# Moving the state products of one attention step behind matmuls of the next layer

## The chip, the core, the metric

One core of a Trainium2 chip runs the whole kernel. The metric is the time of one execution on the device in microseconds (us), as the median of several executions. The profile is one further execution, and its span runs from the first to the last instruction. The engines are called PE (matmuls), DVE (vector), ACT (scalar) and POOL (GpSimd); PSUM is what the kernel calls the memory that its matmuls write (`Sps`, `OK`, `Hps`).

## The reference

A linear attention with decay goes over sequences of 768 rows in blocks and carries a state per head. Its output is the input of a two-layer perceptron with a GELU.

```python
for b in range(nb):                                   # blocks of 64 rows
    intra = einsum('bhic,bhjc->bhij', qb, kb) * Dmask
    intra = einsum('bhij,bhjd->bhid', intra, vb)
    inter = einsum('bhid,bhde->bhie', qb * lam_pow, kv_state)
    out[:, :, sl] = intra + inter
    kv_state = lam_block * kv_state + einsum('bhsd,bhse->bhde', kb_dec, vb)
...
x = out.transpose(0, 2, 1, 3).reshape(B * S, H * D)   # 3072 x 512
return gelu(x @ w_in) @ w_out                          # 512 -> 2048 -> 512
```

## The kernel before

The kernel takes 256 rows of four heads as a step. Steps 0 to 3 make the x of the first 512 rows. Four parts of a step matter here, all on the matmul engine (PE): the scores (`Sps`), the products of k and v that update the state (`OK`, columns 256 and up), the products of v with the masked scores (`PT`), and the products of q with the state `u`. The last two add up x in PSUM, and `x_out` copies it out, half on ACT and half on DVE.

```python
def products(n, s, banks=None, evacuate=True):
    ...
    if n is not None:                 # state products of step n, 16 small matmuls
        ...
    for hp in range(2):               # v with masked scores of step s, 16 small matmuls
        ...
    for c in range(2):                # what the states add, 4 matmuls at step 3
        u = us.pop((s, 0) if c else (s - 2, 1))
        ...
    if evacuate:
        x_out(s, OK)
```

The perceptron's work stands in a queue of pieces, and `fill(n)` issues the next n. For the first 512 rows, the first 16 pieces are four stages of two matmuls each for hidden blocks 0 to 3 (128 of the 2048 hidden columns each). A matmul has 256 columns, so a stage is 8 matmuls. Stages 1 and 2 read the x of steps 0 and 2, stage 3 that of step 1, and stage 4 that of step 3. This is the stretch that the change edits:

```python
update(2, 1, "t")
scores(3)
banks = products(3, None)                      # state products of step 3
cast_win(0, 0, 256, 128, c01)                  # weights of hidden blocks 0, 1 to f16, DVE
cast_win(0, 256, 512, 256, c01, on_act=True)   # blocks 2, 3, ACT
update(3, 0)                                   # new state: DVE, then POOL
causal(3)                                      # mask the scores: DVE
queue_group(0)
fill(8)                                        # stages 1 and 2
cast_win(0, 0, 256, 256, c23, on_act=True)
cast_win(0, 256, 512, 256, c23)
fill(2)                                        # first half of stage 3
products(None, 3, banks, evacuate=False)       # PT, then states
x_out(3, banks[0], nc.vector)
fill(6)                                        # second half of stage 3, stage 4
...
for m in W_SUMS:                               # five sums of w_out weights on DVE
    sum_wout(0, m, DVE)
fill(8)
...                                            # casts of w_out
fill(9)
prep(4)                                        # q of step 4 on DVE, k on ACT
stage_t(4)                                     # transposes of step 4 on PE
```

Of the kernel before, what the change touches and what calls it, by code (L numbers as in the profile page):

```python
# [8 lines left out]
FP32 = mybir.dt.float32  # L9
# [6 lines left out]
def kernel(  # L16
# [12 lines left out]
    P = 128  # L29
    B, H, S, D = q.shape  # L30
    SB = 256
    NSB = S // SB
# [23 lines left out]
    ps_M = ctx.enter_context(tc.tile_pool(name="psM", bufs=6, space=PSUM))  # L56
# [43 lines left out]
    def cast_win(j, lo=0, hi=512, w=256, cs=slice(0, NC), on_act=False):  # L100
        t = wstage[("i", j)]
        for i in range(lo, hi, w):
            dst = w_in16[:, cs, j * 512 + i : j * 512 + i + w]
            src = t[:, cs, i : i + w]
            if on_act:
                pin(nc.scalar.activation(out=dst, in_=src, func=AF.Copy))
            else:
                pin(nc.vector.tensor_copy(out=dst, in_=src))
# [103 lines left out]
    qkT = {}  # L212
# [63 lines left out]
    def half64(i):  # L276
        return slice(64 * i, 64 * i + 64)
# [3 lines left out]
    def scores(n):  # L281
        o = qkT[n]
        Sps = ps_S.tile([P, 2, 2, 2, P], FP32, tag="S", name="Sps")
        for hp in range(2):
            for jk in range(2):
                for hl, c in TILES:
                    pin(nc.tensor.matmul(  # L287
                        Sps[half64(c), hl, hp, jk, :], o[half64(hl), 1, jk, hp, half64(c)],
                        o[half64(hl), 0, :, hp, half64(c)], start=True, stop=True,
                        skip_group_check=True))  # L290
        Ss[n] = Sps

    def causal(n):

        t = ptp.tile([P, 2, 2, 2, P], FP16, tag="PT", name=f"PT_{n}")
        pin(nc.vector.tensor_tensor(  # L296
            t[:].rearrange("p a b c d -> p (a b) (c d)"),
            Ss.pop(n)[:].rearrange("p a b c d -> p (a b) (c d)"),
            mask[:].unsqueeze(1).to_broadcast([P, 4, 2 * P]), ALU.mult))
        PTs[n] = t  # L300

    def products(n, s, banks=None, evacuate=True):


        OK, opened = banks or ([ps_M.tile([P, 512], FP32, tag="M", name=f"OK{c}")
                                for c in range(2)], set())

        def start(c, hl):
            if (c, hl) in opened:
                return False  # L310
            opened.add((c, hl))
            return True

        if n is not None:
            _, tk, tv = a16[n]
            last = (n // 2) % NSB == NSB - 1
            for jk in range(2):
                for hp in range(2):
                    for c, hl in TILES:
                        if c == 1 and last:  # L320
                            continue
                        pin(nc.tensor.matmul(  # L322
                            OK[c][half64(hl), 256 + hp * D : 256 + hp * D + D],
                            tk[half64(c), jk, 2 * hp + hl, :], tv[half64(c), jk, 2 * hp + hl, :],
                            start=start(c, hl), stop=(jk == 1), skip_group_check=True))
            Kps[n] = OK
        if s is None:
            return OK, opened
        sbg, half = divmod(s, 2)
        o = qkT.pop(s)  # L330
        PT = PTs.pop(s)
        _, _, tv = a16.pop(s)
        for hp in range(2):
            for jk in range(2):
                for c, hl in TILES:
                    pin(nc.tensor.matmul(  # L336
                        OK[c][half64(hl), hp * P : hp * P + P], tv[half64(c), jk, 2 * hp + hl, :],
                        PT[half64(c), hl, hp, jk, :], start=start(c, hl), stop=False,
                        skip_group_check=True))
        for c in range(2):  # L340
            if c == 0 and sbg % NSB == 0:
                continue
            u = us.pop((s, 0) if c else (s - 2, 1))
            for hp in range(2):
                pin(nc.tensor.matmul(OK[c][:, hp * P : hp * P + P], u[:, hp].rearrange("p l d -> p (l d)"),  # L345
                                     o[:, 0, :, hp, half64(c)], start=False, stop=True,
                                     skip_group_check=True))
        if evacuate:
            x_out(s, OK)
        return OK, opened  # L350

    def x_out(s, OK, second=None):
        sbg, half = divmod(s, 2)
        g, i = group_of[sbg]
        if g not in xT:
            xT[g] = xtp.tile([P, 2, len(groups[g]), 2, SB], FP16, tag="xT", name=f"xT_{g}")
        dst = xT[g][:, half, i]
        for c in range(2):
            d = dst[:, :, c * P : (c + 1) * P].rearrange("p hp (t j) -> p hp j t", j=2)
            o = OK[c][:, 0:256].rearrange("p (hp j t) -> p hp j t", hp=2, j=2)  # L360
            if c == 1 and second is not None:
                pin(second.tensor_copy(out=d, in_=o))
            else:
                pin(nc.scalar.activation(out=d, in_=o, func=AF.Copy))  # L364
# [3 lines left out]
    def update(s, c, parts="tu"):  # L368


        sbg, half = divmod(s, 2)
        sb = sbg % NSB
        if c == 1 and sb == NSB - 1:
            Kps.pop(s)
            return
        if "t" in parts:
            OK = Kps[s] if c == 0 else Kps.pop(s)
            K = OK[c][:, 256:384].rearrange("p (hp d) -> p hp d", hp=2)
            t = ucp.tile([P, 2, D], FP32, tag=f"t{half}", name=f"t_{s}_{c}")
            if sb == 0 and c == 0:  # L380
                pin(nc.vector.tensor_copy(out=t[:], in_=K))
            else:
                for hp in range(2):
                    pin(nc.vector.scalar_tensor_tensor(  # L384
                        t[:, hp, :], state[half][:, hp, :],
                        lamu[:, 2 * half + hp : 2 * half + hp + 1], K[:, hp, :],
                        ALU.mult, ALU.add))
            state[half] = t
        if "u" in parts:
            u = ubp.tile([P, 2, 2, D], FP16, tag=f"u{half}", name=f"u_{s}_{c}")  # L390
            pin(nc.gpsimd.tensor_tensor(  # L391
                u[:], state[half][:].unsqueeze(2).to_broadcast([P, 2, 2, D]),
                lumask[:, 2 * half : 2 * half + 2, :].unsqueeze(3).to_broadcast([P, 2, 2, D]),
                ALU.mult))
            us[(s, c)] = u
# [196 lines left out]
    def fill(n):  # L592
        for _ in range(min(n, len(filler))):
            filler.pop(0)()

    def R(n, s):
        if n is not None:
            scores(n)
        products(n, s)
        if n is not None:  # L600
            causal(n)
        if s is not None and s % 2 == 1:
            g, i = group_of[s // 2]
            if i == len(groups[g]) - 1 and g > 0:
                queue_group(g)
        if n is not None:
            update(n, 0)
# [18 lines left out]
    prep(2)  # L626
    scores(1)
    products(1, 0)
    causal(1)
    idle(1)  # L630
# [4 lines left out]
    idle(3)  # L635
    scores(2)
    products(2, None)
    update(2, 0)
    causal(2)
# [4 lines left out]
    products(None, 2)  # L644
    update(2, 1, "t")
    scores(3)
    banks = products(3, None)
    c01, c23 = slice(0, 2), slice(2, 4)
    cast_win(0, 0, 256, 128, c01)
    cast_win(0, 256, 512, 256, c01, on_act=True)  # L650
    update(3, 0)
    causal(3)
    queue_group(0)
    fill(8)
    cast_win(0, 0, 256, 256, c23, on_act=True)
    cast_win(0, 256, 512, 256, c23)
    fill(2)
    products(None, 3, banks, evacuate=False)
    x_out(3, banks[0], nc.vector)
    fill(6)  # L660
    update(3, 1, "t")
    cast_win(1, 0, 512, 256, c01)
    cast_win(1, 0, 512, 256, c23)
# [85 lines left out]
```

## Time and profile before

| | kernel before |
|---|---|
| median of 3 | 205.72 us (205.68 to 205.74) |
| span of the profiled execution | 203.7 us |
| PE busy | 196.1 us, 96% |
| PE waits over 0.15 us up to the last matmul | five, 3.8 us together |

PE is nearly always at work. What it waits for in single places, and what stands in those places, decides the time. The lines are in the prediction.

### The profile page before, as it was taken

The numbers are of one execution on the slowest core, as the hardware profiler recorded it, in microseconds if no ns is written. First come the engines' busy times: TensorE is split into PE (matmuls) and PEld (weight loads), VectorE is DVE, ScalarE is ACT, GpSimd is POOL, SyncE is SP. The second block draws the span as 40 slices with busy tenths as digits, with TensorE's granted clock in tenths as the row PEclk, the third lists the DMA queues.
The fourth block names the chain that finished last, engine by engine and source line by source line (L and its number), as shares of the span: only waits on it lengthen the run. The fifth ranks groups of instructions, "written<-read, shape, count | busy, mean of one in ns | idle before, by whom it ended". The sixth has DMA issues, their size and how long they took to land.

```text
span 203.7 us, 5592 instructions
## 1 busy us (share of the span) xinstructions
PE 196.1 (96%) x2324; PEld 128.3 (63%) x2324; DVE 145.3 (71%) x274; ACT 107.6 (53%) x204; POOL 68.4 (34%) x80
## 2 busy tenths in 40 slices
PE   6988999999999999999999999999999999999992
PEld 1556544556875798644688654788554788545882
DVE  5887727877699998929997728996739673136652
ACT  3374778475782573477632477641576431676110
POOL 6594132446576851336134404314412100000000
PEclk9999999999999999999999999999999999999999
DMA  6999999999999999996449993648330003300014
GB/s 173 290 331 386 386 388 373 289 280 303 323 235 230 290 252 170 234 287 170 103 120 249 188 281 101 159 102 133 95 89 0 3 0 103 108 0 0 3 52 155
DMA packets 63945, 37.85 MB, mean 186 GB/s; under 512 B 17584, under 2 KB 59056, under 8 KB 63920
## 3 DMA queue, kind: packets, MB, share of 16 engines
q1 hardware_dynamic: 63088, 36.97, 69.7%
q10 hardware_dynamic: 832, 0.52, 0.9%
q8 instruction: 18, 0.29, 0.6%
q14 instruction: 7, 0.06, 0.1%
HBM read 27.26 MB, written 6.29 MB: 165 GB/s over the span
## 4 chain that ended last, share of the span: by engine, by line
PE 91%; DVE 4%; POOL 1%; issue 1%; ACT 1%; DVEq 0%
PE Hps L419 37%; PE O2ps L434 10%; PE MB L488 8%; PE MA L488 7%; PE MD L488 7%; PE MC L488 4%; PE Sps L287 4%; PE OK L345 3%; PE Hps L534 3%; PE OK L336 3%; PE Tps L258 2%; PE OK L322 1%; DVE PT L296 1%; POOL dq L186 1%; PE idle L152 1%
## 5 line engine op out<-in xcount | busy, mean ns | idle before, releaser
L419 PE MATMUL Hps<-xT,w_in 128*128 128x512 f16 (+1 forms) x416 | 79.1, 347 | 0.0
L423 ACT ACTIVATE gT<-Hps 128x512 f16<-128x512 f32 x88 | 52.1, 597 | 21.9 <-PE Hps L419 21.1
L419 PEld LDWEIGHTS <-w_in 128*128 128x128 f16 x416 | 40.2, 98 | 33.5
L391 POOL TENSOR_TENSOR u<-t,lumask 128x256 f16<-128x256 f32 x40 | 31.3, 789 | 81.2 <-DVE t L384 54.1
L464 DVE TENSOR_TENSOR gs<-gT 128x512 f16<-128x512 f16 (+1 forms) x70 | 36.6, 586 | 10.8 <-ACT gT L423 10.6
L296 DVE TENSOR_TENSOR PT<-Sps,mask 128x1024 f16<-128x1024 f32 x24 | 29.2, 1216 | 16.9 <-PE Sps L287 16.8
L488 PEld LDWEIGHTS <-gs 128*128 128x128 f16 x360 | 34.8, 98 | 4.0
L227 POOL TENSOR_TENSOR v<-v,dv 128x512 f16<-128x512 f32 x24 | 29.0, 1210 | 5.3 <-DMA v<-in_v_dram 1.7
L364 ACT ACTIVATE xT<-OK 128x256 f16<-128x256 f32 x47 | 18.1, 454 | 20.1 <-PE OK L345 16.3
L434 PE MATMUL O2ps<-w_out,gT 128*128 128x512 f16 x96 | 21.9, 379 | 0.0
L495 ACT ACTIVATE m<-MB 128x512 f32<-128x512 f32 x9 | 5.4, 597 | 25.4 <-PE MB L488 25.4
L242 ACT ACTIVATE qk<-k 128x512 f16<-128x512 f32 x24 | 15.0, 626 | 7.0 <-DMA k<-in_k_dram 6.9
L237 DVE TENSOR_TENSOR qk<-q,dq 128x512 f16<-128x512 f32 x23 | 18.4, 799 | 0.0
L488 PE MATMUL MA<-w_sum,gT 128*128 128x256 f16 x144 | 17.5, 273 | 0.1
L488 PE MATMUL MD<-w_sum,gs 128*128 128x256 f16 x136 | 17.5, 273 | 0.0
L488 PE MATMUL MB<-w_out,gs 128*128 128x256 f16 x144 | 17.2, 273 | 0.0
L488 PEld LDWEIGHTS <-gT 128*128 128x128 f16 x144 | 14.0, 98 | 2.8 <-ACT gT L423 0.3
L384 DVE SCALAR_TENSOR_TENSOR t<-t,lamu,OK 128x64 f32<-128x64 f32 x64 | 14.6, 273 | 1.4 <-PE OK L322 0.8
L434 PEld LDWEIGHTS <-gT 128*128 128x128 f16 x96 | 9.2, 98 | 9.9
L499 DVE TENSOR_TENSOR o<-MA,m 128x512 f32<-128x512 f32 x9 | 6.2, 688 | 12.7 <-ACT m L495 12.7
L124 DVE TENSOR_TENSOR w_sum<-wo,wo 128x1024 f16<-128x1024 f32 x6 | 8.8, 1506 | 4.6 <-DMA wo<-in_moe_w_out_dram 4.6
L287 PEld LDWEIGHTS <-qkT 64*64 64x64 f16 x384 | 6.3, 108 | 8.7 <-issue 4.2
(60 smaller groups left out, 168.4 us busy)
## 6 DMA issues: line engine op xcount, KB each, us to landing
q<-in_q_dram SPq DMA_DIRECT2D x24, 256.0 KB, 4.8
k<-in_k_dram SPq DMA_DIRECT2D x24, 256.0 KB, 5.0
v<-in_v_dram SPq DMA_DIRECT2D x23, 256.0 KB, 5.3
out_dram<-o SPq DMA_DIRECT2D x22, 256.0 KB, 4.3
wo<-in_moe_w_out_dram SPq DMA_DIRECT2D x4, 1024.0 KB, 9.1
wi<-in_moe_w_in_dram SPq DMA_DIRECT2D x4, 512.0 KB, 7.8
wi<-in_moe_w_in_dram SPq DMA_DIRECT2D x2, 1024.0 KB, 12.8
v<-in_v_dram ACTq DMA_DIRECT2D x1, 256.0 KB, 4.2
```

Of the source, the lines that this page charges most:

```text
L227: pin(nc.gpsimd.tensor_tensor(wide(tv[:]), ld32[s][2][:], decay(dv, s), ALU.mult))
L237: pin(q_eng.tensor_tensor(wide(tq), q32[:], decay(dq, s), ALU.mult))
L242: pin(nc.scalar.activation(out=wide(tk), in_=k32[:], func=AF.Copy))
L296: pin(nc.vector.tensor_tensor(t[:].rearrange("p a b c d -> p (a b) (c d)"), Ss.pop(n)[:].rearrange("p a b c d -> p (a b) (c d)"), mask[:]. ...
L364: pin(nc.scalar.activation(out=d, in_=o, func=AF.Copy))
L384: pin(nc.vector.scalar_tensor_tensor(t[:, hp, :], state[half][:, hp, :], lamu[:, 2 * half + hp : 2 * half + hp + 1], K[:, hp, :], ALU.mult ...
L391: pin(nc.gpsimd.tensor_tensor(u[:], state[half][:].unsqueeze(2).to_broadcast([P, 2, 2, D]), lumask[:, 2 * half : 2 * half + 2, :].unsqueez ...
L419: pin(nc.tensor.matmul(by_block(Hps[:, i, :]), w_in16[:, c, f * P : (f + 1) * P], x(c), start=(c == 0), stop=(c == NC - 1)))
L423: pin(nc.scalar.activation(out=dst, in_=Hps[:], func=AF.Gelu_apprx_tanh))
L434: pin(nc.tensor.matmul(O2[tau][0][:], gT[:, f % HF, f // HF, tau * P : (tau + 1) * P], w_out16[:, f, :], start=(n == 0), stop=(n == NF - 1)))
L464: pin(nc.vector.tensor_tensor(gsum[m][:, i, :], block(T0, F0, i), block(T1, F1, i), op))
L488: pin(nc.tensor.matmul(dst, lhsT, rhs, start=(i == 0), stop=(i == HF - 1), skip_group_check=True))
```

## The change

The intent is to use two idle moments of PE. The state products of step 3 go behind stage 1, since PE waited 0.73 us in the middle of them. The products with the states go behind the second half of stage 3, so that the states have more time to become ready.

```diff
-    banks = products(3, None)
+    banks = bank_pair()
     c01, c23 = slice(0, 2), slice(2, 4)
     cast_win(0, 0, 256, 128, c01)
     cast_win(0, 256, 512, 256, c01, on_act=True)
-    update(3, 0)
     causal(3)
     queue_group(0)
-    fill(8)
+    fill(4)
+    products(3, None, banks)
+    update(3, 0)
+    fill(4)
     ...
     fill(2)
-    products(None, 3, banks, evacuate=False)
+    products(None, 3, banks, evacuate=False, add_states=False)
+    fill(2)
+    from_states(3, banks[0])
     x_out(3, banks[0], nc.vector)
-    fill(6)
+    fill(4)
```

The rest of the diff splits `products` into the functions that this needs (`bank_pair`, `from_states`) and moves source lines, so L345, L322 and L534 of before are L354, L324 and L540 after.

More of the change, by code (lines that the diff above doesn't have):

```diff
@@ L300, in causal, with bank_pair, products @@
         PTs[n] = t
-    def products(n, s, banks=None, evacuate=True):
-        OK, opened = banks or ([ps_M.tile([P, 512], FP32, tag="M", name=f"OK{c}")
-                                for c in range(2)], set())
+    def bank_pair():
+        return [ps_M.tile([P, 512], FP32, tag="M", name=f"OK{c}") for c in range(2)], set()
+    def products(n, s, banks=None, evacuate=True, add_states=True):
+        OK, opened = banks or bank_pair()
         def start(c, hl):
@@ L328, in products @@
             return OK, opened
-        sbg, half = divmod(s, 2)
-        o = qkT.pop(s)
         PT = PTs.pop(s)
@@ L339, in products, with from_states @@
                         skip_group_check=True))
+        if add_states:
+            from_states(s, OK)
+        if evacuate:
+            x_out(s, OK)
+        return OK, opened
+    def from_states(s, OK):
+        o = qkT.pop(s)
         for c in range(2):
-            if c == 0 and sbg % NSB == 0:
+            if c == 0 and (s // 2) % NSB == 0:
                 continue
@@ L347, in products @@
                                      skip_group_check=True))
-        if evacuate:
-            x_out(s, OK)
-        return OK, opened
     def x_out(s, OK, second=None):
```

## The prediction

> **What bounds the kernel now.** I read the page's busy shares first, then the chain of work that ended last, then every wait of the matmul engine, and last the timelines of 16 to 22 us, the only stretch that the change touches.
>
> The page, busy shares and queues:
>
> ```profile
> PE 196.1 (96%) x2324; PEld 128.3 (63%) x2324; DVE 145.3 (71%) x274; ACT 107.6 (53%) x204; POOL 68.4 (34%) x80
> ...
> PEclk9999999999999999999999999999999999999999
> ...
> q8 instruction: 18, 0.29, 0.6%
> ...
> PE 91%; DVE 4%; POOL 1%; issue 1%; ACT 1%; DVEq 0%
> ```
>
> PE is busy 96% of the span at full clock, and 91% of the chain is PE. So only a PE hole that is closed can shorten the run, and one opened lengthens it. The waits of PE, in us:
>
> ```profile
> PE idle L152 <- DVE ones L146: 1.5, 1, 1.5
> PE OK L322 <- issue: 0.7, 1, 0.7
> PE OK L336 <- DVE PT L296: 0.6, 1, 0.6
> PE Sps L287 <- DVE qkT L263: 0.5, 1, 0.5
> PE Tps L258 <- POOL dq L186: 0.5, 1, 0.5
> ```
>
> The second is what the change aims at: it falls inside the state products of step 3 (L322), and "issue" means that the profile shows nothing that PE waited for. The chain of work between 16 and 26 us (start, length, what):
>
> ```profile
> 16.25 0.35 PE Sps L287 x16
> 16.60 0.03 PE OK L322 x3
> 16.62 0.73 issue
> 17.35 0.31 PE OK L322 x13
> 17.66 2.29 PE Hps L534 x20
> 19.95 0.35 PE OK L336 x16
> 20.30 0.34 PE OK L345 x4
> 20.64 0.02 issue
> 20.66 0.46 DVE xT L362
> 21.12 0.05 issue
> 21.17 4.50 PE Hps L534 x24
> ```
>
> Two weak places stand here: 0.73 us with three products done and thirteen to go, and 0.53 us (20.64 to 21.17) in which x of step 3 is copied out of PSUM before the last first-row pieces may read it. The second is partly covered: four matmuls of other pieces run in it, though the chain does not name them. The PE timeline, and the casts that the first pieces read:
>
> ```profile
> 17.59 2.36 PE L534 MATMUL Hps<-xT,w_in 128*128 128x256 f16 x20
> 19.88 0.42 PE L336 MATMUL OK<-PT,v 64*64 64x128 f16 x16
> 20.23 0.40 PE L345 MATMUL OK<-qkT,u 128*128 128x128 f16 x4
> ```
> ```profile
> 16.08 0.85 DVE L108 CAST w_in<-wi 128x256 f16<-128x256 f32 x2
> 16.79 0.61 ACT L106 ACTIVATE w_in<-wi 128x512 f16<-128x512 f32 x1
> ```
>
> After 21.17 us PE shows no wait over 0.15 us until its tail, so whatever this stretch gains or loses should reach the end nearly whole.
>
> [...] consecutive starts of L534 with 256 columns are 0.109 us apart. The 274 ns of one record is not its cost in a stream; starts are what I count. [...] The page has 18 packets and 0.29 MB on q8, which is 16 KB a packet; the packet records put the first at 14.9 to 16.0 us, and the DMA is busy through all of 16 to 18 us. The instruction that starts at 17.35 has no semaphore to wait for. That fits a late block of instructions, but no view says whose block that packet was. [...]
>
> **The change part by part.** No instruction is added or removed; bytes and tiles stay. On PE the order from the end of the scores (16.60) to the copying out becomes: 8 matmuls of the first four pieces, 16 state products, 8 + 4 matmuls, 16 products with PT, 4 matmuls, 4 products with the states. Before, it was 16 state products, 20 matmuls, 16 with PT, 4 with the states, and 4 matmuls behind them.
>
> Costs, start to start from the PE timeline: a 256-column matmul 0.109. Twenty of them up to the next group took 17.59 to 19.88 = 2.29, so passing into a group of 64-row products costs 2.29 - 20 x 0.109 = 0.11 more. Thirteen state products 17.35 to 17.59 = 0.24; sixteen about 0.27 (estimate). PT products 19.88 to 20.23 = 0.35. From the first states product to the first matmul that may read the new x: 20.23 to 21.17 = 0.94.
>
> *First pieces.* They do not wait for step 3, but for cast weights. DVE's two casts (blocks 0 and 1) end at about 16.5 and 16.93, so blocks 0 and 1 can run in the old hole: 4 matmuls, 0.44 us. Blocks 2 and 3 need the ACT cast, which ends at 16.79 + 0.61 = 17.40 and which the diff does not move (ACT copies out step 2 before it). So block 2 starts at about 17.44 whether or not the unexplained stall is still there. If the stall is a late instruction block, it falls on the same place of the stream, six instructions past the scores, so after three of these matmuls; the fourth then starts at 17.35 and block 2 at 17.46. Both give the same schedule to 0.02 us. I chose 17.44.
>
> *To the states.* Block 2 and 3: 17.44 + 0.44 = 17.88; into the state products +0.11 = 17.99; they take 0.27, 18.26; twelve matmuls 1.31 and +0.11, 19.68; PT products, 20.03; four matmuls, 20.47. Here the first states product starts, 0.24 later than the 20.23 of before. x is then ready 0.94 later, at 21.41 instead of 21.17.
>
> The same as a ledger: 4 matmuls put into the first hole save 0.44; the second start, 17.44 for 17.35, costs 0.09; three more state products 0.03; one more passage into 64-row products 0.11; and the 4 matmuls that used to run behind the copying out now run before it, 0.44 of lost cover. Sum: -0.44 + 0.09 + 0.03 + 0.11 + 0.44 = +0.23 us. This is the core of the prediction: the change fills one hole from work that was already filling another.
>
> *Off the path.* DVE masks step 3 at once (16.93 to about 18.1) instead of after the state update, so PT is early; it was not waited for (19.30 against 19.88) and earns nothing. The update of the state comes at about 18.3 instead of 17.69, and POOL, which needs 0.6 us for one u, has it by about 19.5; the states product at 20.47 does not wait. The DVE cast that followed at 19.22 ends some 0.4 us earlier, which lets the first w_out load be issued a little earlier than 19.78; the casts of w_out are used well after they land, so that moves nothing.
>
> **The rivals.** *The stall was a wait that the new order hides in full* (a state product waiting for v or for a bank). Against it: POOL made v by 16.00, and three products had run already. For it: "issue" may hide a cause that I cannot see. Even then the ACT cast holds block 2 to 17.44, so the time stays at +0.2. Only if blocks 2 and 3 were also ready early, which needs ACT's cast 0.4 us sooner, would the states start near 20.05 and the time be 205.5.
>
> *The copying out stays covered.* If PE could run later pieces past the waiting ones, the 0.44 of lost cover would vanish, giving about 205.5. Against it: matmuls run in the order of the program here, and the next in order are the four that need this x; the trace has PE stop at 20.9 for the same reason even now.
>
> *A new wait for u or for instructions.* If POOL or DVE got to the state of step 3 later than I think, or a fetch met the busy DMA at another place, 0.3 to 0.7 us more: 206.2 to 206.6. The slack for u is about 0.9 us, so I give this little.
>
> *Absorbed later.* The loads and casts of w_out and of steps 4 and 5 have their own pace from 28 to 42 us. If PE arrived at them with no slack, a later PE would lose nothing, and the time would stay at 205.7. But PE shows no wait there, so it sets the pace, and a delay should pass through.
>
> **Range and chances.** 205.72 + 0.23 = 205.95; for the rivals that end at 205.5 to 205.7, I put 205.9. All of them lie within 0.5% of the time before. The three runs span 0.06 us[...]. A range of 205.5 to 206.3 holds the main case and the two likelier rivals. A difference of 2% would be 4.1 us, more than all PE waits listed above together (3.8 us), so "within 2%" has 0.98.
>
> **What would show each step.** Right: in the changed profile the four matmuls of blocks 0 and 1 lie between 16.6 and 17.4, block 2 starts at about 17.4, state products at about 18.0, PT products at about 19.7, states at about 20.5; a wait of PE on the copying out of x of 0.5 us or more just before 21.4, now listed among PE's waits; no idle of PE after it; the waits listed for DVE's state update longer by half a microsecond, without effect. Wrong: the last first-row stage starting before 21.1; a wait on POOL's u; the 0.7 us stall in full, before any matmul of the first pieces; or a span that differs from this stretch's shift by over 0.15 us, which would mean that a later stage took up or added to it.

The marked gaps are passages that no trace or run of this case shows. The ledger is -0.44 + 0.09 + 0.03 + 0.11 + 0.44 = +0.23 us, built on the 0.109 us between starts that the trace of before shows. The 0.3 to 0.7 us for a new wait was the author's estimate; the longest wait without a releaser in that trace was 0.73 us. What another chip may add, cut from the range, was not shown when it was written; in the five calls of this study the medians of the kernel before were 205.44 to 205.73 us.

## The result, and the profile after

| | before | changed |
|---|---|---|
| median of 4 executions each, same chip | 205.73 us (205.68 to 206.18) | 205.61 us (205.40 to 205.81) |
| ratio, 95% interval | | 0.9989 (0.9971 to 1.0007) |
| profiled execution: span | 203.7 us | 204.0 us |
| first score product of step 3 to first matmul of stage 4 | 16.18 to 21.17, 4.99 us | 16.32 to 21.53, 5.21 us |

A ratio is the mean time of one kernel's fast runs over that of the other's of the same rounds, so it is not quite the ratio of the medians. Differences of times are taken before rounding. By the timed runs the two kernels cannot be told apart, since the interval holds 1. The profiled executions are not: the changed kernel is slower by 0.22 us in the stretch, and its start happened to be 0.14 us later. The chain of work of the changed kernel (start, length, what):

```profile
16.96 0.61 PE Hps L540 x4
17.57 0.03 issue
17.61 0.61 PE Hps L540 x4
18.21 0.25 PE OK L324 x16
18.46 1.42 PE Hps L540 x12
19.88 0.35 PE OK L336 x16
20.23 0.54 PE Hps L540 x4
20.77 0.24 PE OK L354 x4
21.01 0.02 issue
21.03 0.45 DVE xT L368
21.48 0.04 issue
21.53 4.50 PE Hps L540 x24
```

This is the predicted sequence. Four matmuls run in the old hole, block 2 begins at 17.61 behind ACT's cast (it ended at 17.55), and the state products follow. At the end PE stands still from 21.01 to 21.53, because the next matmuls in its order read x, which DVE copies out from 21.03 to 21.48. PE's list of waits names it, and has also a small wait of 0.2 us for the first weights (L108):

```profile
PE Hps L540 <- DVE xT L368: 0.5, 1, 0.5
```

The wait of 0.7 us in the state products is gone, and a wait of 0.5 us has come in its place. The state was no issue. POOL made two `u` from 19.06 to 20.36 us in this trace, of which the first is the one asked for, and the products with it began at 20.61:

```profile
19.06 1.30 POOL L397 TENSOR_TENSOR u<-t,lumask 128x256 f16<-128x256 f32 x2 [2.31 <-DVE t L390]
```

### The profile page after: what moved, and what is told of

Read it like the earlier page. It is cut to its first block, busy times and chain, and to the rows that moved or that the text cites. A ratio compares the mean times of both kernels' runs of the same rounds, so it can differ in the third digit from the quotient of the medians.

```text
span 204.0 us, 5592 instructions
## 1 busy us (share of the span) xinstructions
PE 195.2 (96%) x2324; PEld 127.2 (62%) x2324; DVE 145.0 (71%) x274; ACT 108.5 (53%) x204; POOL 69.0 (34%) x80
## 4 chain that ended last, share of the span: by engine, by line
PE 89%; SPq 4%; DMA 3%; DVE 1%; issue 1%; ACT 1%
PE Hps L425 37%; PE O2ps L440 10%; PE MB L494 8%; PE MA L494 7%; PE MD L494 7%; SPq L69 4%; PE MC L494 4%; PE Hps L540 4%; PE Sps L287 3%; DMA wi<-in_moe_w_in_dram 3%; PE OK L354 3%; PE OK L336 3%; PE OK L324 1%; PE Tps L258 1%; PE ME L494 0%
```

## The experiments

Twelve runs were made, on three chips. All were correct.

| run | median us | before | ratio, 95% interval |
|---|---|---|---|
| first half of the change alone | 205.35 | 205.46 | 0.9994 (0.9971 to 1.0017) |
| second half alone | 205.41 | 205.46 | 0.9998 (0.9972 to 1.0025) |
| eight matmuls behind the copying out | 205.35 | 205.46 | 0.9991 (0.9964 to 1.0018) |
| instruction stream shifted | 205.93 | 205.46 | 1.0014 (0.9990 to 1.0038) |
| before, against itself | 205.39 | 205.45 | 0.9996 (0.9984 to 1.0008) |
| changed kernel again | 205.87 | 205.45 | 1.0021 (1.0004 to 1.0038) |
| eight matmuls, fifth sum later | 204.98 | 205.45 | 0.9981 (0.9964 to 0.9999) |
| before, fifth sum later | 204.79 | 205.44 | 0.9959 (0.9938 to 0.9981) |
| eight matmuls, fifth sum later, again | 204.98 | 205.44 | 0.9967 (0.9942 to 0.9991) |
| eight matmuls, again | 205.36 | 205.44 | 0.9990 (0.9968 to 1.0012) |
| before, fifth sum later, again | 204.81 | 205.44 | 0.9976 (0.9954 to 0.9998) |
| changed kernel, fifth sum later | 205.98 | 205.44 | 1.0022 (1.0004 to 1.0040) |

### First half alone

```diff
-    products(None, 3, banks, evacuate=False, add_states=False)
-    fill(2)
-    from_states(3, banks[0])
+    products(None, 3, banks, evacuate=False)
     x_out(3, banks[0], nc.vector)
-    fill(4)
+    fill(6)
```
(against the changed kernel)

> Only the first half of the change: the state products of step 3 stand behind the first four pieces, but the products with the states follow those with PT at once, and two pieces (4 matmuls) run behind the copying out again. I measure from the first score product of step 3 to the first matmul of the last first-row stage (4.99 us before, 5.21 in the changed kernel), which leaves out what the start of the program varies by. My theory (a hole filled, 0.44 us of cover lost): the 0.44 comes back, so 4.77 us, 0.22 less than before, and a total 0.2 us under the kernel before (ratio 0.999). Rival, that pieces behind the copying out do not matter: 5.2 us and the time of the changed kernel. No wait of 0.7 us within the state products in either.

The stretch took 16.33 to 21.10 = 4.77 us, as expected to the hundredth. Four matmuls are again behind the copying out, and PE's timeline shows no wait there:

```profile
20.16 0.40 PE L354 MATMUL OK<-qkT,u 128*128 128x128 f16 x4
20.39 1.31 PE L540 MATMUL Hps<-xT,w_in 128*128 128x256 f16 x8
```

The total moved by less than its interval.

### Second half alone

```diff
     fill(2)
-    products(None, 3, banks, evacuate=False)
+    products(None, 3, banks, evacuate=False, add_states=False)
+    fill(2)
+    from_states(3, banks[0])
     x_out(3, banks[0], nc.vector)
-    fill(6)
+    fill(4)
```
(against the kernel before)

> Only the second half: state products directly after the scores as before, but two pieces moved from behind the copying out to before the products with the states. My theory: the unexplained wait of 0.7 us stands among the state products as before, and 0.44 us of cover is lost, so 4.99 + 0.44 = 5.43 us on the same stretch, and a PE wait of about 0.5 us on the copying out; total 0.4 us over the kernel before (ratio 1.002). Rival, that the second half takes away a wait on POOL's u: 5.0 us or less. If the 0.7 us wait was a chance of one execution, it will be missing here and the stretch will be 0.5 to 0.7 us shorter.

The wait among the state products is there again, after the same three, and it is shorter:

```profile
16.23 0.20 PE L324 MATMUL OK<-v,qk 64*64 64x64 f16 x3
16.91 0.31 PE L324 MATMUL OK<-v,qk 64*64 64x64 f16 x13 [0.48 <-issue]
...
21.15 2.13 PE L540 MATMUL Hps<-xT,w_in 128*128 128x256 f16 x13 [0.54 <-DVE xT L368]
```

So the whole stretch took 5.17 us, not 5.43. Counted from the end of that wait to stage 4 it is 21.15 - 16.91 = 4.24 us, against 21.17 - 17.35 = 3.82 before. The second half alone costs 0.42 us, against 0.44 in the ledger. The two halves add up: measured from the first score product, -0.22 and +0.44 (5.21 - 4.77) give the +0.22 of the whole change. The total, expected at a ratio of 1.002, was 0.9998 and does not show the loss.

### Eight matmuls behind the copying out

```diff
-    fill(2)
-    products(None, 3, banks, evacuate=False, add_states=False)
-    fill(2)
-    from_states(3, banks[0])
+    products(None, 3, banks, evacuate=False)
     x_out(3, banks[0], nc.vector)
-    fill(4)
+    fill(8)
```
(against the changed kernel)

> The first half of the change, with the opposite of the second: all four pieces (8 matmuls, 0.87 us) of the third stage run behind the copying out. By my ledger the products with the states may start about 0.87 us earlier than in the changed kernel, x is ready 0.94 us after their start, and 8 matmuls cover it whole: the last stage starts 4.5 us after the first score product (5.21 in the changed kernel, 4.99 before), no PE wait on the copying out of step 3, total 0.4 to 0.5 us under the kernel before (ratio 0.998). Rival: the products with the states then wait for POOL's u, which in the changed kernel was ready about 19.7 us; a PE wait on POOL of 0.2 us or more, and 4.7 us or more on the stretch. Rival, cover does not matter: 5.2.

The stretch took 15.94 to 20.47 = 4.52 us, so the ledger held again, and no wait on POOL came up. But the trace kept little of this lead to its end, and the ratio of 0.9991 with its interval does not show the expected 0.998. From stage 4 to the last matmul the kernel before, the changed kernel and both halves each took 178.64 us; this one took 179.23. The lead was lost at the first transposes of step 4, as the timelines of PE and DVE around 40 us show:

```profile
40.06 0.62 PE L258 MATMUL Tps<-ident,qk 128*128 128x128 f16 x8 [0.43 <-DVE qk L237]
```
```profile
37.35 2.05 DVE L124 TENSOR_TENSOR w_sum<-wo 128x1024 f16<-128x1024 f32 x1
39.32 0.68 DVE L237 TENSOR_TENSOR qk<-q,dq 128x512 f16<-128x512 f32 x1
```

DVE makes q of step 4 only after five sums of w_out weights, which begin when the second w_out load lands (DVE waited 4.61 us for it). However early PE had come in this execution, it could not have passed 40.06 us; below this is called the wall. Its place is not the same in every execution: two timed ones of this kernel had spans of 203.2 and 203.3 us against 203.5 here. In the kernel before, PE came at 40.18 and saw nothing of this.

### Instruction stream shifted

```diff
     update(1, 1, "t")
-    idle(3)            # three matmuls of 512 columns into a scratch bank
+    idle_narrow(12)    # twelve of 128 columns
```
(against the kernel before)

> The kernel before, with one edit that changes no time on paper: three idle matmuls of 512 columns, ahead of the scores of step 2, become twelve of 128, which take as long but are 18 more instructions (a weight load and a matmul each). If the unexplained wait is a block of instructions that comes late, it sits at a fixed count of the instruction stream and so must move 18 instructions forward: out of the state products and into the scores of step 3, after about 10 of 16, with a length of 0.7 to 1.0 us and no semaphore; total as before within 0.2 us. If it is a wait of the fourth state product for its data or its bank, it stays there with three of sixteen done. If it was chance, it is missing and the total is 0.5 to 0.7 us less.

That the twelve take as long was an estimate: at the 0.216 us between starts of 512 columns (L419) and 0.056 of 128 (L345) in the trace of before, it is 0.65 against 0.67 us. A weight load for each matmul is what the page of before shows (2324 of each).

The wait moved exactly as far as the stream was shifted, out of the state products and behind ten of the sixteen score products:

```profile
15.83 0.35 PE L292 MATMUL Sps<-qkT 64*64 64x128 f16 x10
16.34 0.30 PE L292 MATMUL Sps<-qkT 64*64 64x128 f16 x6 [0.15 <-issue]
16.43 0.34 PE L327 MATMUL OK<-v,qk 64*64 64x64 f16 x16
```

It was shorter than expected, and its end kept to something else: the first 16 KB packet of the instruction queue. The table takes the landings from the trace's packet records and the other times from the starts of single instructions.

| trace | first instruction packet landed | PE went on | between |
|---|---|---|---|
| before | 16.02 | 17.35 | 1.33 |
| second half alone | 15.54 | 16.91 | 1.37 |
| stream shifted | 14.92 | 16.34 | 1.42 |
| before, against itself | 16.08 | 17.38 | 1.30 |
| first half alone | 16.09 | 17.39 | 1.30 |

In the last row the place is the one that the prediction named for the new order, after three matmuls of the first pieces: their starts were 16.93, 17.05, 17.16, then 17.39. A fixed count in the stream, no releaser that the profile shows, and an end tied to a packet fit a late block of instructions, and neither rival explains the move. No view names the engine that a packet is for. That it was PE's is inferred: the page of before has 18 such packets, and PE has 4648 of its 5592 instructions (2324 matmuls and 2324 weight loads), against 274 on DVE, the next. The total was expected unchanged within 0.2 us. The median is 0.47 us higher, but the ratio of 1.0014 has an interval that holds 1. This trace also met the wall at the transposes (40.06 us).

### The kernel before against itself

> The kernel before, unchanged, run as if it were a new one: what a comparison of a kernel with itself gives here. Ratio 1.000; its interval is the smallest that any of these comparisons can be trusted to. In the profile a wait of PE without a semaphore after three of the sixteen state products of step 3, of any length from 0 to 0.8 us, that ends 1.3 to 1.4 us after the first 16 KB packet of the instruction queue has been moved (1.33 us in the kernel before, 1.37 with the second half alone, 1.42 with the stream shifted). If the wait is something else, its end will not keep to that distance.

The ratio was 0.9996 with an interval of 0.0012 to either side, so a difference under 0.25 us is not to be read from such totals. The wait cost less here, since it ended at 17.38 (17.35 in the first trace) while the scores came later (16.80 for 16.18): the third and fourth state products started 0.33 us apart. So the stretch from the first score product to stage 4 took 16.80 to 21.21 = 4.42 us in this execution, against 4.99 in the first trace of the same kernel. PE's timeline has the first of these times, the chain of work the second:

```profile
16.80 0.42 PE L287 MATMUL Sps<-qkT 64*64 64x128 f16 x16
```
```profile
21.21 1.91 PE Hps L534 x12
```

### The changed kernel again

> The changed kernel again: the stretch from the first score product of step 3 to the last first-row stage takes 5.2 us again (within 0.03), with a PE wait of 0.5 us on the copying out of step 3. From the start of that last stage to the last matmul 178.64 us, as in four traces so far. The total differs from the kernel before by less than the interval.

The stretch took 5.67 us, not 5.2: a miss. This execution had an early start, so PE stood before the first pieces, whose weights were not cast:

```profile
15.50 0.42 PE L287 MATMUL Sps<-qkT 64*64 64x128 f16 x16
16.80 1.05 PE L540 MATMUL Hps<-xT,w_in 128*128 128x256 f16 x8 [0.89 <-DVE w_in L108]
...
21.16 1.05 PE L540 MATMUL Hps<-xT,w_in 128*128 128x256 f16 x8 [0.54 <-DVE xT L368]
```

From block 2's first matmul to stage 4 it took 17.25 to 21.16 = 3.91 us, as in the first trace (17.61 to 21.53 = 3.92). In the kernel before the same piece takes 3.13 us (18.04 to 21.17), and 3.12 to 3.14 in all five traces with its order of work. The order of the work has a fixed cost; what precedes it does not. From stage 4 to the last matmul it was 178.64 us, as expected. The total was expected within the interval and was not: 1.0021 with 1.0004 to 1.0038 is just clear of 1. The start of a trace varies: the first score product of step 3 came anywhere from 15.49 to 16.97 us in the fourteen traces.

### Eight matmuls behind, and the fifth sum of DVE later

```diff
-    for m in W_SUMS:
+    for m in list(W_SUMS)[:4]:
         sum_wout(0, m, DVE)
     ...
     prep(4)
+    sum_wout(0, 6, DVE)
     stage_t(4)
```
(against the kernel with eight matmuls behind)

> The kernel with eight matmuls behind the copying out, which gained 0.47 us by the last first-row stage and lost 0.59 us of its lead at the first transposes of step 4 (40.06 us), where PE waited for DVE's product of q of step 4, itself behind five sums of w_out weights. Here the fifth sum stands behind that product. If this queue on DVE is what takes the gain back, the product of q ends at about 38.6 to 39.2, the transposes start at 39.3 to 39.5 instead of 40.06, and the last matmul comes at 199.0 to 199.2 instead of 199.69: 0.5 to 0.6 us less than with eight matmuls behind alone, about 0.6 us less than before (ratio 0.997). If instead k of step 4 lands too late (ACT's cast of it ended at 39.4), the transposes start at 39.4 to 39.5 all the same. Rival, that a DMA of q lands as late as DVE asks for it: the transposes stay at 40.0 and nothing is gained.

The profile fell on a late start (16.76), so PE came to the transposes at 40.28 and nothing of the wall could show: the expected 39.3 to 39.5 was missed for that reason. DVE had q at 38.8. The timed runs moved as expected in direction, 204.98 us, though by 0.2% and not 0.3%.

### The control: the kernel before with the fifth sum later

The edit is the one above, made to the kernel before.

> The kernel before with the fifth w_out sum of DVE behind the product of q of step 4, and nothing else. A control for the reordering: in the kernel before PE came to the first transposes of step 4 at 40.18 us, after DVE had q (39.98), so there is 0.1 to 0.2 us to gain at most, and only in executions whose start is early. I expect a ratio of 0.999 to 1.000, and 178.64 us from the last first-row stage to the last matmul as before. If the reordering alone gives the 0.4 us that it gave together with the eight matmuls, the ratio is 0.998 and my floor story is wrong.

This expectation was wrong, and it is the run that taught most. The reordering alone gives 204.79 us, ratio 0.9959, and every one of its six runs (204.59 to 205.09) is under the fastest of the eleven of before (205.21). The eight matmuls behind the copying out show no gain beyond it (0.9981 and 0.9967). The trace is one with an early start:

```profile
15.57 0.42 PE L287 MATMUL Sps<-qkT 64*64 64x128 f16 x16
15.81 0.29 PE L322 MATMUL OK<-v,qk 64*64 64x64 f16 x16
16.81 1.38 PE L534 MATMUL Hps<-xT,w_in 128*128 128x256 f16 x11 [0.70 <-DVE w_in L108]
...
39.40 0.61 PE L258 MATMUL Tps<-ident,qk 128*128 128x128 f16 x8
...
63.67 0.26 PEld L287 LDWEIGHTS <-qkT 64*64 64x64 f16 x16 [0.57 <-DMA qkT<-qk]
```

The instruction packet landed at 14.20, early enough, and the sixteen state products ran without a break in time in which PE had to wait for the first weights anyway. Stage 4 began at 20.39 and the transposes at 39.40, before the 40.06 that the five sums allowed in the other trace. The expected 178.64 us was missed: from stage 4 to the last matmul it took 178.78 us here and 178.90 in the repeat, since the earlier PE met a second wall. The last line shows it: the weights for score products wait for a DMA that transposes q and k.

### Both versions with eight matmuls again

> Eight matmuls behind the copying out and the fifth sum behind q, again: its profile last time fell on an execution with a late start (first score product of step 3 at 16.76 us), so the floor could not show. From block 2's first matmul to the last first-row stage 3.24 us, as in both traces with eight matmuls behind (3.92 in the changed kernel). If this execution starts early, the transposes of step 4 come before 40.0 us, with no PE wait over 0.2 us there, and 178.64 us again from the last stage to the last matmul; ratio 0.998.

> Eight matmuls behind the copying out, the sums as they were, again on the same chip as the one with the sum moved: slower than that one by 0.2 to 0.4 us in the median where starts are early, since the transposes of step 4 cannot start before 40.0 us; ratio to the kernel before 0.999. Rival: both the same, and the difference between them last time was chance.

With the sum moved 204.98 us, without it 205.36 (204.70 to 205.56 against 205.21 to 205.81): a difference of 0.38 us in the medians, as earlier (205.35 and 204.98, on different chips). The intervals of the two ratios overlap, so this pair alone does not rule out chance; the two runs of the kernel before with the sum moved weigh more. Both profiles fell on late starts (16.79 and 16.97) and show no wall; from block 2's first matmul to stage 4 both took 3.23 to 3.24 us.

### With and without the change once the wall is gone

> The kernel before with the fifth sum behind q, again: the ratio of 0.996 that I had not expected should repeat if the first transposes of step 4 hold up the kernel before in most executions (those with an early start), and is 1.000 if it was chance. I expect 0.996 to 0.998, with no PE wait on DVE's q at the transposes of step 4.

> The changed kernel with the fifth sum behind q. With the floor at the transposes of step 4 out of the way, what the change does to its own stretch should reach the end. In traces with an early start the last first-row stage came at 21.16 us in the changed kernel and at 20.39 in the kernel before with the sum moved: there the state products ran while PE had to wait for the first weights anyway, and behind four pieces they cost their full time. So I expect this kernel 0.3 to 0.8 us slower than its counterpart without the change (early starts 0.77, late ones 0.2): near 205.4, ratio to the kernel before about 1.000. Rival: the change costs nothing even so, and both are at 204.8 (ratio 0.996 or 0.997). From block 2's first matmul to the last stage 3.92 us again.

On one chip, both with the fifth sum later: 204.81 us without the change, 205.98 with it. The ratios to the kernel before, 0.9976 and 1.0022, give 1.0022 / 0.9976 = 1.0046, or 0.9 us, a little above the expected 0.3 to 0.8; with both intervals, taken as independent, it is about 0.4 to 1.5 us. Part of it is how the executions fell. Without the change four took 204.59 to 204.87 us and two 205.68 to 205.87; with it two took 205.42 to 205.48 and four 205.96 to 206.36. Between the lower groups the change costs 0.7 us, between the upper ones 0.4. The profiled executions, both with an early instruction packet (14.16 and 14.07), differ by 21.22 - 20.34 = 0.88 us at stage 4, and by 199.86 - 199.24 = 0.62 us at the last matmul, because the kernel without the change lost 0.26 at the second wall. From block 2's first matmul to stage 4 the changed one took 3.92 us, as expected. PE waits 0.5 us for DVE's copy of x in it again. The trace of the other has no such wait. It spends 0.7 us at the first weights instead, with the state products already done.

## Why the prediction was right or wrong

**The time and the class** were right: 205.61 us, and 205.87 on another chip, lie in the range of 205.5 to 206.3, well within 2%. The range held the likelier rivals too, so the hit does not choose among them.

**The ledger** gave the right sum for the two profiled executions, +0.23 us against +0.22, and its costs are confirmed: the lost cover is 0.42 to 0.44 against 0.44. Its saving is not a property of the kernels, and here the close agreement is partly luck. After block 2's first matmul the change costs 3.92 - 3.13 = 0.79 us in every trace of the two orders. What it can win is an earlier start of block 2, counted from the first score product of step 3. In the first pair that was 1.28 against 1.86 us, 0.58 won. In the other trace of the unchanged kernel block 2 came after 1.28 us as well, nothing was won, and against that trace's stretch of 4.42 us the changed kernel's 5.21 is 0.79 longer. With early starts it was 1.75 us against 1.69 and 1.73 (the latter two with the fifth sum later), and nothing was won either.

**The first pieces** kept to ACT's cast, as predicted, at 17.61 rather than 17.44, because ACT copied out step 2 0.14 us later in that execution.

**The unexplained wait** fits a late block of instructions: it ended 1.30 to 1.42 us after the first packet of the instruction queue in five traces. The prediction offered this without settling it, and said that for its sum it did not matter. That holds for the schedule of the changed kernel, but not for what it is compared with. The prediction took the 0.73 us of one execution for a fixed length, and this is what failed in the ledger: the hole to be filled was that long in one trace alone. It was 0.48 us in the second half's trace, 0.15 in the shifted one, 0.14 in the kernel before against itself, and absent where the packet came at 14.2.

**One sign failed without harm.** DVE's wait before the state update was to grow by half a microsecond. It fell from 0.8 to 0.3 us, because the masking of the scores now stands before it on DVE.

**What failed is the step "a delay should pass through", with "PE shows no wait there, so it sets the pace".** In the two profiles it is true: 178.64 us from stage 4 to the last matmul in both. In general it is not. The wall at the transposes of step 4 stood only some 0.1 us ahead of PE in the profile of before: DVE had q at 39.98 and PE came at 40.18, while in the trace that shows the wall these were 40.00 and 40.06. An earlier PE hits it. The prediction had it as the rival "absorbed later" and dismissed it from the one trace, in which PE was just late enough to see no wait. The wall is shown in two traces, those with eight matmuls behind and with the shifted stream. That the kernel before meets it in most timed executions is inferred: moving one sum took 0.5 to 0.8 us off it twice, and of the 44 executions of the kernel before none took under 205.16 us, while 10 of the 12 with the sum moved did. No trace caught the kernel before at it.

**So the change cost more in the stretch than predicted in all but the first pair of traces, and less of it reached the end when the start was early.** Without the wall, an early start costs 16.80 to 21.16 = 4.36 us from the first piece to stage 4, against 16.81 to 20.39 = 3.58: 0.78 us, of which 0.44 is the lost cover and about 0.34 the state products, which were free before the weights came. With the wall, the kernel before can't use all of its lead. So the two kernels end close together (how much each kind of start counts in the timed runs is not shown): the medians of the changed one were 0.12 us below and 0.42 us above those of before (0.9989 and 1.0021). What the change does to the total is not settled more closely than by these two intervals, from 0.3% less to 0.4% more; that it makes the kernel slower once the wall is gone rests on one pair of runs.

**The best version found** is the kernel before with one DVE sum moved behind q of step 4: 204.79 and 204.81 us, 0.24 to 0.41% under the kernel before. It does not contain the change.

## What to carry to other kernels

Matmuls put into one hole come out of another place; ask what they were covering there, here the copying out of PSUM that the next pieces need. Before trusting that a gain passes to the end, look for engines whose results come just before the busy one asks for them: a slack of 0.1 us shows as no wait at all, and is a wall for the next improvement. And read more than one execution where the start varies, since the same kernel can have its idle time in different places: a wait of 0.73 us among the state products in one trace of the kernel before, of 0.14 us in the other.

## What the traces show of PE's costs

- PE stood up to 0.73 us where a block of instructions seems to have come late, and went on 1.30 to 1.42 us after the first 16 KB packet had landed, in five traces. The busy share of the DMA engines was 1.05 from 16 to 18 us in the trace of before, and the wait there came after 446 matmuls and weight loads (register and semaphore instructions not counted). That the packets were PE's is inferred from their number and the table above.
- In streams the starts were 56 ns apart for 128 columns (L345), 109 for 256 (L534) and 216 for 512 (28 matmuls of L419 in 6.04 us), though the record of one of 256 columns lasts 273 ns.
- From the start of the last 256-column matmul to the first 64-row product behind it was 0.203 us in the traces of before and of the changed kernel, 0.09 more than the 0.109 within the group.
